# High and low parts of K and Q made in place, five steps ahead, with only the second head's rows moved

## The chip, the cores and the metric

One core of a Trainium2 chip runs the whole program. TensorE multiplies matrices, VectorE and ScalarE work on tiles in SBUF and PSUM, GpSimd works on tiles in SBUF, and SyncE (SP) issues the transfers: loads from HBM and moves from one place in SBUF to another. All of SP's transfers run on the core's 16 DMA engines. The metric is the device time in microseconds, the median of several runs.

## The reference

Attention with a forget gate over 4 batches x 8 heads, 576 positions, head size 64, and two feed-forward layers behind it over all 2304 positions:

```python
scores = scale * np.matmul(q, k.transpose(0, 1, 3, 2))
cum = np.cumsum(np.log(np.clip(f, 0.0001, 1.0)), axis=-1)
decay = cum[:, :, :, None] - cum[:, :, None, :]
scores = np.where(causal, -1e9, scores + decay)      # causal: above the diagonal
attn = softmax(scores)                               # row by row
x = attn @ v                                         # heads side by side: (2304, 512)
h = x @ w_in;  x = (h - tanh(h)) @ w_out             # w_in 512x2048, w_out 2048x512
h = x @ w2_in; out = silu(h) @ w2_out
```

All in float32. The kernel splits each factor of a product into a high part and a low part (the rest), and adds the products high x high, high x low and low x high.

## The kernel before, in words

**Pairs and steps.** The 32 heads are worked on as 16 pairs (two heads, 64 partitions each). A pair is nine tiles of scores: four row blocks of head 0, one tile that holds the last 64 rows of both heads, four row blocks of head 1. One loop takes one tile per step, and within a step each engine has work of several tiles: at step n TensorE transposes tile n-9 and computes the scores of tile n+2, ScalarE takes the exponentials of tile n-1, VectorE the row minimum of tile n and the evacuation of transposed tiles, GpSimd normalises tiles n-5 to n-3 every third step. So the normalised tiles are wanted by TensorE four steps later at the soonest, and pair p's first score is at step 9p-2. PSUM has three buffers for transposed tiles (`ps_t`): TensorE can transpose a new one only when VectorE has evacuated the third before it.

**Operands of the scores.** From pair 2 on, a score tile is two matmuls, one of `kqa` (`ta`) and one of `kqb` (`tb`), each [128, 2 heads, 1280 columns], K in columns 64 to 639, Q behind it. For head h, `ta` holds in its upper 64 partitions the high parts of K and Q, in its lower 64 the low part of K and the high part of Q; `tb` holds the high part of K and the low part of Q, and in partitions 64 to 67 four rows of decay. There are two sets (`kqt`), used by even and odd pairs. Pairs 0 and 1 use the same memory in another form (`plain`): whole high and low parts side by side, four matmuls a tile.

**How a pair is prepared.** `load_kq` loads K and Q of both heads in one transfer into `kqraw` (two buffers). `split(p, 0)` and `split(p, 1)` cast the high part into `kqhi` (K on GpSimd, Q on VectorE), `split(p, 2..5)` subtract it for the low part into `kqlo` (GpSimd, four pieces). `kqhi` and `kqlo` have one buffer each. `place` then moves the parts by DMA, six moves out of `kqhi` and four out of `kqlo`, to their places in `ta` and `tb`, and two transfers bring the decay rows from DRAM (`dec`). A table (`prep`) gives for each of these the step, relative to step 9p, at which the work for pair p+1 is issued; each engine runs its own instructions in the order of issue. A pair's operand set is free when the pair before the previous one has had its last score, at step 9p-3; head 0's half of it is free from step 9p-6 on, when the tile with the last rows is through.

**The other transfers on SP's queue.** At step 9p+1 the K/Q load of two pairs on, at step 9p+6 a V load (three buffers; it waits for the values' matmuls of an older pair), and at steps 27, 36, 45, 54, 90, 99, 135, 137 one 512 KB load of feed-forward weights each. SP issues strictly in order: an instruction that waits holds up all that stand behind it. Each transfer also uses one of eight semaphores in turn, and so waits for the eighth before it.

Of the kernel before, what the change touches and what calls it, by code (L numbers as in the profile page):

```python
# [8 lines left out]
F32R = mybir.dt.float32r  # L9
# [5 lines left out]
P = 128  # L15
# [25 lines left out]
def forgetting_attention_two_ffn(  # L41
# [286 lines left out]
    def attention():  # L328
        with ExitStack() as actx:
# [18 lines left out]
            NP = B * NPAIR  # L348
            raw, vraw, kqs, vals = {}, {}, {}, {}
            kqt = []  # L350
            for i in range(2):
                ta = kp.tile([P, 2, W], F32R, name=f"kqa{i}")
                tb = kp.tile([P, 2, W], F32R, name=f"kqb{i}")
                kqt.append((ta, tb))
# [30 lines left out]
            def split(p, j):  # L385
                if p not in kqs:
                    kqs[p] = plain[p][0:2] if p < 2 else [
                        rq.tile([P, RAW], F32R, tag=tag, name=f"{tag}{p}") for tag in ("kqhi", "kqlo")
                    ]
                hi, lo = kqs[p]  # L390
                if j == 0 and p > 1:
                    nc.gpsimd.tensor_scalar(hi[:, 0:S], raw[p][:, 0:S], 1.0, 1.0, ALU.mult, ALU.mult)
                elif j < 2:
                    c = KQ if j == 0 else slice(S, RAW)
                    (nc.vector.tensor_copy if p else nc.scalar.copy)(hi[:, c], raw[p][:, c])
                else:
                    c0, c1 = ((0, 288), (288, S), (S, S + 320), (S + 320, RAW))[j - 2]
                    sub(lo[:, c0:c1], raw[p][:, c0:c1], rd(hi[:, c0:c1]))

# [26 lines left out]
            def place(p, j):  # L426


                ta, tb = (rd(t) for t in kqt[p % 2])
                if j == 2:  # L430
                    src = dec[2 * p:2 * p + 2].rearrange("h r w -> r h w")
                    if p < 4:

                        nc.vector.memset(tb[64:68, :, Z1:Q1], 0.0)
                    nc.sync.dma_start(out=tb[64:68, :, K0:Z1], in_=src[:, :, 0:S + 512])
                    nc.sync.dma_start(out=tb[64:68, :, Q1:W], in_=src[:, :, S + 512:2 * S])
                    return
                for h in range(2):
                    a = rd(kqs[p][j][64 * h:64 * h + 64])
                    if j == 0:  # L440
                        nc.sync.dma_start(out=ta[0:64, h, K0:W], in_=a)  # L441
                        nc.sync.dma_start(out=ta[64:128, h, Q0:W], in_=a[:, S:RAW])  # L442
                        nc.sync.dma_start(out=tb[0:64, h, K0:Q0], in_=a[:, 0:S])
                    else:
                        nc.sync.dma_start(out=ta[64:128, h, K0:Q0], in_=a[:, 0:S])
                        nc.sync.dma_start(out=tb[0:64, h, Q0:W], in_=a[:, S:RAW])

# [222 lines left out]
            for a in pt4:  # L670
# [5 lines left out]
            prep = {  # L676
                -8: [(load_kq, None)], -5: [(split, 0), (split, 1)], -4: [(split, 2)], -3: [(split, 3)],
                -2: [(split, 4), (place, 2), (place, 0)], -1: [(split, 5), (place, 1)],
                10: [(prep_v, 0)], 12: [(prep_v, 1)], 15: [(load_v, None)],
# [11 lines left out]
            for p in range(NP - 1):  # L691
                for k, items in prep.items():
                    for fn, j in items:
                        if fn is prep_v:
                            later(9 * p + k, fn, p + 1, j)
                        elif j is not None:
                            if p:
                                later(9 * p + k, fn, p + 1, j)
                        elif p + 2 < NP and (p or fn is load_v):
                            later(9 * p + k, fn, p + 2)  # L700

# [131 lines left out]
```

## Time and profile before

| | us |
|---|---|
| three timed runs | 1031.77 median (1030.31 to 1033.46) |
| the profiled execution | 1022.97 |
| its span, from the first instruction to the last | 1021.2 |
| TensorE busy in the span | 991.2 (97%) |
| attention in it | about 11 to 235 |

The views answer different questions. The busy line tells which engine is full over the span; the windows tell where it is not; the wait list tells what ended an engine's idle time; the timeline shows one such wait with its neighbours; the chain follows the work that ended last from release to release. "kqhi<-kqraw" is a tile and what it is made from; buffer numbers are left out. An instruction of SP marked SPq is an issue, not a transfer: how long a transfer takes to land is seen from who waited for it.

### The profile page before, as it was taken

What the parts mean: (1) busy time and instruction counts of PE and PEld (TensorE: products, weight loads), DVE (VectorE), ACT (ScalarE), POOL (GpSimd) and SP (SyncE); (2) the same over time, 40 slices, a digit from 0 to 9 for tenths busy, and PEclk for the clock granted to TensorE, in tenths of its full rate; (3) what the DMA queues carried; (4) which work ended last, traced back from release to release, by engine and by line L of the source; (5) the groups of instructions that cost most, each with busy time, mean ns of one, the idle gap of its engine ahead of it and who ended that gap; (6) DMA issues with size and microseconds to landing.
All of it is one profiled execution on the core that took longest, in us unless ns stands there. A gap on an engine that the chain in (4) does not pass through costs nothing.

```text
span 1021.2 us, 14016 instructions
## 1 busy us (share of the span) xinstructions
PE 991.2 (97%) x4944; PEld 828.5 (81%) x4944; DVE 597.1 (58%) x1385; ACT 492.8 (48%) x1094; POOL 202.1 (20%) x288
## 2 busy tenths in 40 slices
PE   5989989999999999999999999999999999999998
PEld 4777777877898888988888888888888888888887
DVE  6677788878686544757466674443453456633323
ACT  4678788885355342434343444343344334433222
POOL 8677888975000000000000000000000000000000
PEclk9999999999999999999999999999999999999999
DMA  5899999812221101111011220110110111001111
GB/s 154 231 256 258 226 234 268 211 49 84 82 83 42 42 1 42 62 63 42 1 42 49 77 83 1 42 41 21 63 42 1 42 42 42 1 1 42 42 41 62
DMA packets 28181, 81.78 MB, mean 80 GB/s; under 512 B 4368, under 2 KB 4368, under 8 KB 28080
## 3 DMA queue, kind: packets, MB, share of 16 engines
q1 hardware_dynamic: 28104, 80.88, 27.0%
q8 instruction: 39, 0.64, 0.3%
q14 instruction: 30, 0.25, 0.1%
q10 hardware_dynamic: 8, 0.02, 0.0%
HBM read 49.39 MB, written 5.31 MB: 54 GB/s over the span
## 4 chain that ended last, share of the span: by engine, by line
PE 85%; DMA 5%; ACT 3%; SPq 2%; POOL 2%; DVE 2%; issue 1%; DVEq 0%; POOLq 0%; ACTq 0%
PE a L315 39%; PE h L256 38%; PE out_t L600 3%; DMA kqb<-kqhi 2%; PE t L555 2%; PE s L473 2%; DMA vraw<-v 1%; ACT p L527 1%; DMA kqb<-kqlo 1%; SPq L441 1%; POOL p L541 1%; PE s L477 1%; SPq L442 1%; ACT pth L573 1%; PE s L476 1%
## 5 line engine op out<-in xcount | busy, mean ns | idle before, releaser
L256 PE MATMUL h<-xh,wh 128*128 128x512 f32 (+1 forms) x640 | 237.2, 371 | 0.0
L256 PE MATMUL h<-xl,wh 128*128 128x512 f32 (+1 forms) x640 | 235.5, 368 | 0.0
L256 PE MATMUL h<-xh,wl 128*128 128x512 f32 (+1 forms) x640 | 235.5, 368 | 0.0
L278 DVE TENSOR_TENSOR gl<-g,gh 128x512 fp32r<-128x512 f32 (+1 forms) x158 | 101.6, 643 | 101.8 <-ACT gh L274 99.8
L274 ACT CAST gh<-g 128x512 fp32r<-128x512 f32 (+1 forms) x160 | 92.6, 579 | 95.9 <-DVE g L271 93.4
L256 PEld LDWEIGHTS h<-xh,wh 128*128 128x128 f32 x640 | 120.7, 189 | 21.1 <-issue 0.7
L256 PEld LDWEIGHTS h<-xl,wh 128*128 128x128 f32 x640 | 120.7, 189 | 21.0 <-issue 0.7
L256 PEld LDWEIGHTS h<-xh,wl 128*128 128x128 f32 x640 | 120.6, 188 | 20.0
L315 PE MATMUL a<-gh,wh 128*128 128x512 f32 (+1 forms) x320 | 117.9, 369 | 0.0
L315 PE MATMUL a<-gl,wh 128*128 128x512 f32 (+1 forms) x320 | 117.8, 368 | 0.0
L315 PE MATMUL a<-gh,wl 128*128 128x512 f32 (+1 forms) x320 | 117.7, 368 | 0.0
L315 PE MATMUL a<-wh,gh 128*128 128x512 f32 x288 | 112.2, 390 | 0.0
L315 PE MATMUL a<-wl,gh 128*128 128x512 f32 x288 | 112.2, 390 | 0.0
L315 PE MATMUL a<-wh,gl 128*128 128x512 f32 x288 | 112.0, 389 | 0.0
L273 ACT ACTIVATE g<-h 128x512 f32<-128x512 f32 (+1 forms) x80 | 44.4, 555 | 113.6 <-PE h L256 98.5
L244 DVE TENSOR_TENSOR xl<-y,xh 128x512 fp32r<-128x512 f32 (+1 forms) x60 | 37.4, 638 | 96.6 <-ACT xh L242 96.6
L242 ACT CAST xh<-y 128x512 fp32r<-128x512 f32 (+1 forms) x60 | 34.2, 580 | 104.8 <-PE h L256 103.1
L527 ACT ACTIVATE p<-p,mn 128x128 f32<-128x128 f32 (+3 forms) x128 | 72.3, 565 | 9.7 <-DVE mn L511 4.8
L541 POOL TENSOR_SCALAR p<-p,sm 128x128 f32<-128x128 f32 (+3 forms) x128 | 69.9, 558 | 22.9 <-DVE sm L538 10.4
L555 PE MATMUL t<-ident,p 128*128 128x128 f32 x320 | 59.6, 285 | 12.7 <-DVE sm L534 9.2
L244 DVE TENSOR_TENSOR xl<-x,xh 128x512 fp32r<-128x512 f32 (+1 forms) x56 | 34.5, 634 | 62.2 <-ACT xh L242 62.2
L315 PEld LDWEIGHTS a<-gh,wh 128*128 128x128 f32 x320 | 60.3, 189 | 10.4 <-ACT x L611 0.4
(127 smaller groups left out, 1690.8 us busy)
## 6 DMA issues: line engine op xcount, KB each, us to landing
raw<-w_in SPq DMA_DIRECT2D x32, 512.0 KB
raw<-w_out SPq DMA_DIRECT2D x32, 512.0 KB
kqraw<-kq SPq DMA_DIRECT2D x16, 608.0 KB
kqa<-kqhi SPq DMA_DIRECT2D x28, 304.0 KB
vraw<-v SPq DMA_DIRECT2D x16, 320.0 KB
out<-ob SPq DMA_DIRECT2D x18, 256.0 KB
kqa<-kqhi SPq DMA_DIRECT2D x28, 160.0 KB
kqb<-kqlo SPq DMA_DIRECT2D x28, 160.0 KB
```

What stands on the lines that cost most here:

```text
L242: nc.scalar.copy(hi[:, :n], src[:, k, t0:t0 + n])
L244: eng.tensor_tensor(lo[:, :n], src[:, k, t0:t0 + n], rd(hi[:, :n]), ALU.subtract)
L256: nc.tensor.matmul(hp[:, :n], w[:, k * P:k * P + P], m[:, :n], start=(k == 0 and r == 0), stop=(k == NKT - 1 and r == 2),)
L273: nc.scalar.activation(g[:, :n], hp[:, :n], AF.Silu)
L274: nc.scalar.copy(gh[:, :n], g[:, :n])
L278: eng.tensor_tensor(gl[:, :n], g[:, :n], rd(gh[:, :n]), ALU.subtract)
L315: nc.tensor.matmul(dst, w, m, start=(first and r == 0), stop=(last and r == 2))
L473: nc.tensor.matmul(s[:, :n], a[:, q], b[:, 0:n], start=r == 0, stop=r == 3)
L527: nc.scalar.activation(pt[:, :w], pt[:, :w], AF.Exp, bias=mn, scale=-1.0, accum_out=sums[:, n // 3 % 5, n % 3, 0:1],)
L541: nc.gpsimd.tensor_scalar(pt[:, :w], pt[:, :w], sm[:, j:j + 1], 1.0, ALU.mult, ALU.mult)
L555: nc.tensor.transpose(tp[:, c, :], pt[:, c * P:c * P + P], ident)
L600: nc.tensor.matmul(dst, w, pt[:, 448 * c + a:448 * c + q1], start=(c == 0 and r == 0), stop=(c == last and r == len(terms) - 1),)
```

## The change

High parts of pairs 2 and up are cast straight into the first head's slot of `ta`, over all 128 partitions: the upper 64 are then in place, and head 1's, in the lower 64, are moved from there. The low part of Q goes in the same way into the first head's slot of `tb`. The low part of K goes into a new tile `klo` (one buffer). `kqhi` and `kqlo` are gone. Eight moves a pair are left of ten, in three groups with the decay rows behind them: `place(p, 0)` moves 1 to 4 (head 1's high parts, and head 0's high K into `tb`), `place(p, 1)` moves 5 and 6 (low K of head 1 and of head 0), `place(p, 2)` moves 7 and 8 (head 1's low Q; head 0's high Q into the lower half), `place(p, 3)` the decay rows. Casts and subtractions keep their count and sizes; one subtraction each is issued a step earlier, the decay rows two steps later. For pairs 2 and 3, whose sets still hold plain operands, all of it is issued three steps later, and so are the K/Q loads that wait for it.

```diff
--- before.py
+++ after.py
@@ -346,8 +346,10 @@
             ps_s = pool(early, "ps_s", 3, space=PSUM)
 
             NP = B * NPAIR
-            raw, vraw, kqs, vals = {}, {}, {}, {}
+            raw, vraw, vals = {}, {}, {}
             kqt = []
+
+            klo = rq.tile([P, S], F32R, name="klo")
             for i in range(2):
                 ta = kp.tile([P, 2, W], F32R, name=f"kqa{i}")
                 tb = kp.tile([P, 2, W], F32R, name=f"kqb{i}")
@@ -383,11 +385,13 @@
                 nc.gpsimd.tensor_tensor(out, a, b, ALU.subtract)
 
             def split(p, j):
-                if p not in kqs:
-                    kqs[p] = plain[p][0:2] if p < 2 else [
-                        rq.tile([P, RAW], F32R, tag=tag, name=f"{tag}{p}") for tag in ("kqhi", "kqlo")
-                    ]
-                hi, lo = kqs[p]
+
+
+                ta, tb = kqt[p % 2]
+                if p > 1:
+                    hi, lo = ta[:, 0, K0:W], (klo, tb[:, 0, Q0:W])
+                else:
+                    hi, lo = plain[p][0], (plain[p][1][:, 0:S], plain[p][1][:, S:RAW])
                 if j == 0 and p > 1:
                     nc.gpsimd.tensor_scalar(hi[:, 0:S], raw[p][:, 0:S], 1.0, 1.0, ALU.mult, ALU.mult)
                 elif j < 2:
@@ -395,7 +399,8 @@
                     (nc.vector.tensor_copy if p else nc.scalar.copy)(hi[:, c], raw[p][:, c])
                 else:
                     c0, c1 = ((0, 288), (288, S), (S, S + 320), (S + 320, RAW))[j - 2]
-                    sub(lo[:, c0:c1], raw[p][:, c0:c1], rd(hi[:, c0:c1]))
+                    b = S * (j > 3)
+                    sub(lo[j > 3][:, c0 - b:c1 - b], raw[p][:, c0:c1], rd(hi[:, c0:c1]))
 
             def split_last(p, j):
 
@@ -426,24 +431,26 @@
             def place(p, j):
 
 
+
                 ta, tb = (rd(t) for t in kqt[p % 2])
-                if j == 2:
-                    src = dec[2 * p:2 * p + 2].rearrange("h r w -> r h w")
-                    if p < 4:
-
-                        nc.vector.memset(tb[64:68, :, Z1:Q1], 0.0)
-                    nc.sync.dma_start(out=tb[64:68, :, K0:Z1], in_=src[:, :, 0:S + 512])
-                    nc.sync.dma_start(out=tb[64:68, :, Q1:W], in_=src[:, :, S + 512:2 * S])
+                top, end = slice(0, 64), slice(64, 128)
+                kk, qs = slice(K0, Q0), slice(Q0, W)
+                moves = (
+                    ((ta[top, 1, K0:W], ta[end, 0, K0:W]), (ta[end, 1, qs], ta[end, 0, qs]),
+                     (tb[top, 1, kk], ta[end, 0, kk]), (tb[top, 0, kk], ta[top, 0, kk])),
+                    ((ta[end, 1, kk], rd(klo[end])), (ta[end, 0, kk], rd(klo[top]))),
+                    ((tb[top, 1, qs], tb[end, 0, qs]), (ta[end, 0, qs], ta[top, 0, qs])),
+                )
+                if j < 3:
+                    for a, b in moves[j]:
+                        nc.sync.dma_start(out=a, in_=b)
                     return
-                for h in range(2):
-                    a = rd(kqs[p][j][64 * h:64 * h + 64])
-                    if j == 0:
-                        nc.sync.dma_start(out=ta[0:64, h, K0:W], in_=a)
-                        nc.sync.dma_start(out=ta[64:128, h, Q0:W], in_=a[:, S:RAW])
-                        nc.sync.dma_start(out=tb[0:64, h, K0:Q0], in_=a[:, 0:S])
-                    else:
-                        nc.sync.dma_start(out=ta[64:128, h, K0:Q0], in_=a[:, 0:S])
-                        nc.sync.dma_start(out=tb[0:64, h, Q0:W], in_=a[:, S:RAW])
+                src = dec[2 * p:2 * p + 2].rearrange("h r w -> r h w")
+                if p < 4:
+
+                    nc.vector.memset(tb[64:68, 1, Z1:Q1], 0.0)
+                nc.sync.dma_start(out=tb[64:68, :, K0:Z1], in_=src[:, :, 0:S + 512])
+                nc.sync.dma_start(out=tb[64:68, :, Q1:W], in_=src[:, :, S + 512:2 * S])
 
             def prep_v(p, j):
                 r = vraw[p].rearrange("p h (c d) -> p c h d", d=D)[:, :, 0, :]
@@ -674,8 +681,9 @@
             scores(tiles[1])
 
             prep = {
-                -8: [(load_kq, None)], -5: [(split, 0), (split, 1)], -4: [(split, 2)], -3: [(split, 3)],
-                -2: [(split, 4), (place, 2), (place, 0)], -1: [(split, 5), (place, 1)],
+                -8: [(load_kq, None)], -5: [(split, 0), (split, 1)], -4: [(split, 2)],
+                -3: [(split, 3), (split, 4)], -2: [(split, 5), (place, 0)], -1: [(place, 1)],
+                0: [(place, 2), (place, 3)],
                 10: [(prep_v, 0)], 12: [(prep_v, 1)], 15: [(load_v, None)],
             }
             due = {}
@@ -694,10 +702,11 @@
                         if fn is prep_v:
                             later(9 * p + k, fn, p + 1, j)
                         elif j is not None:
+
                             if p:
-                                later(9 * p + k, fn, p + 1, j)
+                                later(9 * p + k + (3 if p < 3 else 0), fn, p + 1, j)
                         elif p + 2 < NP and (p or fn is load_v):
-                            later(9 * p + k, fn, p + 2)
+                            later(9 * p + k + (3 if fn is load_kq and p < 4 else 0), fn, p + 2)
 
             parts = (
                 ([(0, 0), (64, 0), (64, 1)], [(64, 2), (64, 3), (64, 4)]),
```

SP's queue as built before, for pair 4 (`dec` are the decay rows; "waits" names the semaphores: an engine's for its instructions, DMAHW0 to 7 for transfers):

```order
L435 DMA kqb_103<-dec 4x2x1088 [waits DMAHW6_49,PE_49]
L436 DMA kqb_103<-dec 4x2x64 [waits DMAHW7_49]
L441 DMA kqa_102<-kqhi_608 64x1216 [waits DMAHW0_49,DVE_49,Pool_49]
L442 DMA kqa_102<-kqhi_608 64x640 [waits DMAHW1_49]
L443 DMA kqb_103<-kqhi_608 64x576 [waits DMAHW2_49]
L441 DMA kqa_102<-kqhi_608 64x1216 [waits DMAHW3_49]
L442 DMA kqa_102<-kqhi_608 64x640 [waits DMAHW4_49]
L443 DMA kqb_103<-kqhi_608 64x576 [waits DMAHW5_49]
L445 DMA kqa_102<-kqlo_609 64x576 [waits DMAHW6_49,Pool_49]
L446 DMA kqb_103<-kqlo_609 64x640 [waits DMAHW7_49,Pool_49]
L445 DMA kqa_102<-kqlo_609 64x576 [waits DMAHW0_49]
L446 DMA kqb_103<-kqlo_609 64x640 [waits DMAHW1_49]
```

And with the change, the same pair's moves 1 to 8, the decay rows, a weight load and a K/Q load:

```order
L446 DMA kqa_103<-kqa_103 64x1216 [waits DMAHW2_49,PE_49,Pool_49]
L446 DMA kqa_103<-kqa_103 64x640 [waits DMAHW3_49]
L446 DMA kqb_104<-kqa_103 64x576 [waits PE_49]
L446 DMA kqb_104<-kqa_103 64x576 [waits DMAHW5_49]
L446 DMA kqa_103<-klo 64x576 [waits DMAHW6_49,Pool_49]
L446 DMA kqa_103<-klo 64x576 [waits DMAHW7_49,DMAHW4_49,DMAHW2_49]
L446 DMA kqb_104<-kqb_104 64x640 [waits DMAHW0_49,Pool_49]
L446 DMA kqa_103<-kqa_103 64x640 [waits DMAHW3_49,DMAHW1_49]
L452 DMA kqb_104<-dec 4x2x1088 [waits DMAHW0_49]
L453 DMA kqb_104<-dec 4x2x64
L141 DMA raw_0_0_713<-w_in 128x1024
L377 DMA kqraw_729<-kq 128x1216 [waits DMAHW5_49]
```

Two moves are gone, the decay rows stand last instead of first, and the sixth move and the first decay transfer wait for the semaphores of moves just issued (DMAHW4 and DMAHW2 are those of moves 3 and 1, the decay's DMAHW0 is that of move 7), not only for the one whose turn it is.

VectorE before, around its cast of pair 6's high Q (`ptl` is an evacuation of a transposed tile, `sm` the row sums, `mn` the minimum):

```order
L511 ISA pt_0_106,mn_2_4_991<-misc,mask_132,mn_2_4_991 128x288 [waits DVE_49,PE_49]
L511 ISA mn_2_4_991 128x1
L395 CAST kqhi_994<-kqraw_740 128x640 [waits DMAHW3_49,DMAHW2_49,DMAHW4_49,DMAHW1_49,DMAHW7_49,DMAHW0_49,Pool_49]
L582 TENSOR_TENSOR ptl<-t_0_3_959,pth 128x4x128 [waits Activation_49]
L534 TENSOR_REDUCE sm_1011<-sums 128x3
```

And with the change:

```order
L518 ISA pt_0_107,mn_2_4_976<-misc,mask_133,mn_2_4_976 128x288 [waits DVE_49,PE_49]
L518 ISA mn_2_4_976 128x1
L399 CAST kqa_103<-kqraw_729 128x640 [waits DMAHW5_49,DMAHW2_49,DMAHW1_49]
L589 TENSOR_TENSOR ptl<-t_0_3_944,pth 128x4x128 [waits Activation_49]
L541 TENSOR_REDUCE sm_994<-sums 128x3
```

The cast stands in the same place. Before, it waited for the six moves out of `kqhi` of the pair before; now for its own load and for two moves of the pair two before, which used the same operand set.

## Rows read from the trace of the kernel before

**Rows 1.** The page, part 1: busy us, share of the span, instructions.
```profile
PE 991.2 (97%) x4944; PEld 828.5 (81%) x4944; DVE 597.1 (58%) x1385; ACT 492.8 (48%) x1094; POOL 202.1 (20%) x288
```

**Rows 2.** Windows: stretch, us, busy us by engine, granted clock, DMA share, GB/s.
```profile
100.00:150.00 50.00, 45.84 (x284) 38.08 (x284) 40.01 (x155) 39.10 (x122) 43.89 (x64) 0.97 0.91 231
200.00:250.00 50.00, 46.73 (x246) 36.70 (x245) 39.57 (x94) 36.14 (x87) 37.34 (x38) 1.00 0.28 92
114.50:117.50 3.00, 3.00 (x12) 2.61 (x12) 2.91 (x15) 0.92 (x3) 3.00 (x5) 0.50 0.68 149
```

**Rows 3.** Waits, 11 to 240 us: who waited for whom; us, times, longest.
```profile
PE t L555 <- DVE sm L534: 9.2, 9, 1.8
...
POOL kqhi L392 <- DMA kqb<-kqhi: 7.6, 4, 3.0
...
DVE kqhi L395 <- DMA kqa<-kqhi: 2.7, 2, 1.9
```

**Rows 4.** Timeline, 111 to 113 us: start, duration, engine, line; idle before, releaser.
```profile
111.69 0.49 DVE L395 CAST kqhi<-kqraw 128x640 fp32r<-128x640 f32 x1 [1.93 <-DMA kqa<-kqhi]
...
112.10 0.68 DVE L582 TENSOR_TENSOR ptl<-t,pth 128x512 fp32r<-128x512 f32 x1
...
112.93 0.41 PE L555 MATMUL t<-ident,p 128*128 128x128 f32 x2 [1.80 <-DVE sm L534]
```

**Rows 5.** Timeline of TensorE: the first score matmul of pairs 2, 3, 14, 15.
```profile
37.26 0.31 PE L476 MATMUL s<-kqa 128*128 128x128 f32 x1
...
48.69 0.31 PE L476 MATMUL s<-kqa 128*128 128x128 f32 x1
...
189.04 0.31 PE L476 MATMUL s<-kqa 128*128 128x128 f32 x1
...
200.44 0.31 PE L476 MATMUL s<-kqa 128*128 128x128 f32 x1
```

**Rows 6.** DMA issues: out<-in, queue, count, KB of each.
```profile
raw<-w_in SPq DMA_DIRECT2D x32, 512.0 KB
...
kqraw<-kq SPq DMA_DIRECT2D x16, 608.0 KB
...
kqa<-kqhi SPq DMA_DIRECT2D x28, 304.0 KB
...
vraw<-v SPq DMA_DIRECT2D x16, 320.0 KB
...
kqb<-kqlo SPq DMA_DIRECT2D x28, 160.0 KB
...
kqb<-kqhi SPq DMA_DIRECT2D x28, 144.0 KB
```

**Rows 7.** Timeline of SP's queue: start and duration of two issues.
```profile
37.09 0.27 SPq L435 DMA_DIRECT2D kqb<-dec  x1
...
44.24 0.59 SPq L445 DMA_DIRECT2D kqa<-kqlo  x1
```

**Rows 8.** Windows of loads alone and of moves alone.
```profile
59.00:62.00 3.00, 2.85 (x20) 2.40 (x19) 3.00 (x16) 2.57 (x10) 2.48 (x6) 1.00 0.96 336
70.00:72.00 2.00, 2.00 (x16) 1.79 (x15) 1.31 (x5) 2.00 (x6) 0.00 (x0) 1.00 0.97 238
```

**Rows 9.** Timeline, first 6 us: two issues, and their first readers.
```profile
0.74 0.39 SPq L633 DMA_DIRECT2D x<-f  x1
...
1.19 0.41 SPq L375 DMA_DIRECT2D kqraw<-kq  x1
...
2.69 0.96 DVE L112 TENSOR_SCALAR x<-x 32x576 f32<-32x576 f32 x1
...
5.46 0.67 ACT L395 CAST kqa<-kqraw 128x576 fp32r<-128x576 f32 x1 [1.10 <-DMA kqraw<-kq]
```

**Rows 10.** The chain in order of time: start, us, what.
```profile
35.89 1.14 PE s L473 x4
...
161.34 3.31 DMA kqb<-kqlo
```

## The prediction, made before the changed kernel was run

> **What bounds the kernel now.** The page first: TensorE is busy 97% of the span [rows 1], so only its idle time can be won, and nearly all of that lies in attention. The windows next: from 100 to 150 us the DMA engines are busy 0.91 of the time at 231 GB/s while TensorE has 45.84 of 50 us, from 200 to 250 us the DMA share is 0.28 [rows 2]. So attention strains the DMA queue, and the two feed-forward layers do not. The wait list then names the wait: VectorE's and GpSimd's casts into `kqhi` wait for transfers that still read that one buffer, and TensorE's transposes wait nine times, 9.2 us in all, for VectorE [rows 3]. One such case in order of time: VectorE's cast idles 1.93 us for a transfer out of `kqhi`, the evacuation of the transposed tile follows behind it, and TensorE stands 1.80 us [rows 4].
>
> Measure the loss by the first score matmul of a pair. From pair 2 to pair 3 a pair takes 48.69 - 37.26 = 11.43 us, and from 14 to 15, with no K/Q load left in the queue, 200.44 - 189.04 = 11.40: TensorE's own pace. From pair 3 to pair 15 it is 200.44 - 48.69 = 151.75 us, where 12 pairs at 11.43 would be 137.2 [rows 5]. So some 14.6 us is what DMA waits cost here, and the change can win no more than that plus small change.
>
> **The change part by part.** *The removed wait.* High parts go into the first head's slot of the pair's own operands. There are two such sets, so the casts of a pair no longer follow the transfers of the pair just before; their readers are a pair older and done. The 14.6 us of lateness loses this cause entirely.
>
> *The transfers.* Before, ten moves a pair: 2 x (304 + 160 + 144 + 144 + 160) KB = 1824 KB. After, eight: 304 + 160 + 144 + 144, then 144 + 144, then 160 + 160 = 1360 KB, a quarter less [rows 6]; the moves out of the low parts have the same two small sizes. Two issues of some 0.6 us each go too [rows 7], on a queue (SP) that is not what TensorE waits for; I count them only where they stand in the loop below. Casts and subtractions keep number and size, so VectorE, ScalarE and GpSimd gain or lose no work; that the subtractions stand one step earlier is covered by GpSimd's normalisations, which have four steps of room.
>
> *What is late next.* The moves now depend on each other. Move 6 (low K of head 0) overwrites rows that moves 1 and 3 read, so SP stands until move 3 has landed. The decay rows overwrite rows that move 7 reads, so SP stands again until move 7 has landed; and the next pair's first score needs those decay rows. Queued behind each standing instruction on SP: the other moves, the weight load, the next K/Q load, the V load, and then the next pair's move 1. Those loads, issued last, are served first of the next round, ahead of move 1. Thus a loop: loads, move 1 to 3 landed, move 6 and 7, move 7 landed, decay rows, loads.
>
> Its price. Rates: two short windows, one with loads and one with moves alone, show 336 and 238 GB/s [rows 8]. The fixed part of a landing, beyond bytes by rate: the first `f` transfer is issued at 0.74 and used at 2.69, so 72 KB take at most 1.95, of which 0.2 is bytes: 1.7 us at most. The first K/Q load, issued at 1.19 and used at 5.46, takes 4.27, of which 0.62 MB by 336 is 1.85: 2.4 us. A 160 KB move late in a row of moves takes 3.31 on the chain, of which 0.69 is bytes: 2.6 us, queueing included [rows 9, 10]. For the loads I take their own 2.4; for moves, where 2.6 has queue in it and 1.7 has not, the middle, 2.1. Then, from the issue of a weight load:
> - loads and move 1 land: 2.4 + (0.524 + 0.623 + 0.328) / 0.336 + 0.311 / 0.238 = 2.4 + 4.4 + 1.3 = 8.1 us
> - moves 2 and 3: (0.164 + 0.147) / 0.238 = 1.3
> - move 6 issued: 0.6 [rows 7]; move 7 lands 2.1 + 0.7 = 2.8 after its issue
> - two decay issues before the next load: 0.6 (one is 0.27 [rows 7])
>
> 13.4 us with a weight load in the round, 11.85 without its 1.56. Both exceed 11.43. Six rounds (after the chains of pairs 4 to 7, 11 and 12, from steps 27, 36, 45, 54, 90, 99) hold a weight load; five hold only K/Q and V; the last, with no K/Q load, runs at TensorE's 11.43. Pairs 3 to 15: 6 x 13.4 + 5 x 11.85 + 11.43 = 151.1 us, against 151.75 before. The old lateness is paid back almost to the microsecond.
>
> *The three steps' delay for pairs 2 and 3.* Their set still holds plain operands. Pair 1's last plain scores end near 35.89 + 1.14 = 37.0 [rows 10]; a cast (0.7 estimated), then 3.4 + 1.3 + 0.6 + 2.8 and the decay rows' 2.6 make 48.4, against a due 48.69 [rows 5]; GpSimd's subtractions may push that back. 0 to 1.5 us late; I take 1. Pair 2 has the longer plain pair before it and costs nothing.
>
> Sum: 151.1 - 151.75 + 1 = +0.4 us (rounded). Past pair 15 nothing differs and the shift carries to the end. The profiled execution took 1022.97 us (span 1021.2), 8.8 under the median of the timed runs, 1031.77; the difference is applied to the median: 1032.
>
> *The clock.* The granted clock is 0.50, the 1.2 GHz level, in 114.5 to 117.5 us [rows 2], just after TensorE had stood 1.80 us [rows 4]. Rounds with a weight load will idle TensorE some 2 us; a fall there slows work that has those 2 us to spare. I put nothing on it.
>
> A rule that speaks against the change: by the Trainium skill, DMA: Bandwidth & Descriptors, Two DMAs through the same engine are not ordered, a transfer that depends on an earlier one has to be held at the issuing engine until the earlier one's semaphore is complete; the queue's order is no substitute. The program's order agrees: move 6 and the decay rows carry such waits. Were order enough, a round would be 5.9 us of moves and 4.4 of loads, under 11.43, and the sum 137.2: 14.6 us faster. I go by the waits.
>
> **The rivals.** *Faster: the moves land quicker than I take.* With 1.7 for every landing a round is 13.4 - 0.7 - 0.4 = 12.3 with a weight load and below TensorE's pace without: 6 x 12.3 + 6 x 11.43 = 142.4, 9.4 us less: 1022. For it: a quarter fewer bytes, and the queue is empty when moves 6 and 7 start. Against it: the load row's 2.4. Chance 0.23.
>
> *Faster still: moves also run at the loads' rate.* With 1.7 per landing and 336 GB/s for every byte a round with a weight load is 1.7 + 4.4 + 0.93 + 0.93 + 0.6 + 1.7 + 0.49 + 0.6 = 11.35 us, under TensorE's pace: all 14.6 us won, 1018 with 1 us lost at pair 3. For it: a move alone in the queue was not seen. Against it: the 238 GB/s of the window with moves alone [rows 8]. Chance 0.03. Beside it stands the Trainium skill, DMA: Bandwidth & Descriptors, Anatomy of one DMA, whose fit (made on another issue path) is 2.0 us plus bytes at 436 GB/s; by it, as an estimate, a round is 10.4 us.
>
> *Slower: the chain of landings outweighs the removed wait.* Place: TensorE's first score of each pair, standing for the decay rows. With 2.6 for every landing a round is 13.4 + 0.2 + 0.5 = 14.1, and 12.55 without a weight load; the sum is 6 x 14.1 + 5 x 12.55 + 11.43 = 158.8, 7 us more, and with 1.5 at pair 3 8.5 us: 1040. For it: 3.31 for a small move [rows 10]; every hiccup of the queue now lies on the chain. It decides from 0.14 us more per landing (two landings in each of 11 rounds: 3.1 us). Chance 0.31.
>
> *The wait moves instead of going:* VectorE's cast still waits for its pair's K/Q load, now issued behind the decay rows. That load is issued some 2 us before a pair's first score and lands in some 4.3 [rows 9], 6 behind a weight load; the cast needs it six steps of 11.43 / 9 us, 7.6 us, after that score. Some 3.5 us to spare; it would cost about 1.5 us in each of ten rounds, 1047, if not. Chance 0.03.
>
> **How the numbers follow.** No change to be told (within 0.3%, 3.1 us, about what this kernel's measurement can tell from none): 0.40, itself 1029 to 1035. Faster 0.23 + 0.03 = 0.26, slower 0.31 + 0.03 = 0.34. The range takes in both ends of the landing time: 1023 to 1041.
>
> **What would show it.** Right: no wait of VectorE's or GpSimd's casts for a move; TensorE's waits at the first score of a pair, ended by the decay transfer; SP standing on its own transfers twice a pair; pair periods near 13.4 and 11.9; DMA share down to some 0.8. Wrong for the size: periods of 11.4 throughout (landings quicker), or over 12.5 without a weight load (slower). Wrong altogether: casts that still wait for transfers, or stalls at pairs 2 and 3 alone.

## The result, and the profile after

| | us |
|---|---|
| before, 4 timed runs | 1031.04 median (1025.1 to 1033.46) |
| changed, 4 timed runs | 1043.06 median (1041.33 to 1046.1) |
| ratio | 1.015, 95% interval 1.011 to 1.019 |
| predicted | 1032, range 1023 to 1041 |
| profiled execution of the changed kernel | 1041.33, span 1039.5 |

Slower by 1.5%, and outside the range. In a later comparison it was 1038.01 against 1028.05: 1.0098 (1.0072 to 1.0125).

The page's first line answers to [rows 1]: TensorE has 10 us more busy time (much of it at half speed, below) and 8 us more idle time.

```profile
PE 1001.2 (96%) x4944; PEld 834.4 (80%) x4944; DVE 597.0 (57%) x1385; ACT 491.0 (47%) x1094; POOL 199.5 (19%) x288
```

The first window of [rows 2] after the change (stretch, us, busy us of TensorE, its weight loads, VectorE, ScalarE, GpSimd, granted clock, DMA share, GB/s):

```profile
100.00:150.00 50.00, 42.95 (x266) 34.74 (x266) 37.72 (x149) 38.01 (x120) 39.19 (x57) 1.00 0.74 182
```

From 100 to 150 us the DMA engines are less busy than before, 0.74 against 0.91, and TensorE has less to do as well, 42.95 against 45.84 us. A quarter fewer moved bytes, and more waiting: something stands still between the transfers. The waits from 11 to 240 us (three of TensorE's, then SP's two longest; us, times, longest) say what:

```profile
PE s L484 <- DMA kqb<-dec: 14.3, 11, 1.9
PE s L480 <- POOL kqa L385: 3.1, 1, 3.1
...
PE t L562 <- DVE sm L541: 1.5, 5, 0.5
...
SPq L446 <- DMA kqb<-kqa: 33.3, 14, 5.0
SPq L452 <- DMA kqb<-kqb: 19.9, 14, 1.6
```

The 9.2 us behind VectorE of [rows 3] are down to 1.5, and no cast waits for a move. In their place TensorE stands eleven times, 14.3 us, at a pair's first score for the decay rows; SP stands once a pair for move 3 (in front of move 6) and once for move 7 (in front of the decay rows). The chain in order of time, the two links of it in one round:

```profile
75.36 2.54 DMA kqb<-kqb
77.90 0.02 issue
77.92 2.68 DMA kqb<-dec
...
80.73 0.30 PE s L484
...
90.04 2.97 DMA kqb<-kqb
93.01 0.02 issue
93.02 2.70 DMA kqb<-dec
```

Move 7 lands, the decay rows are issued 0.02 us later and land, the score starts 0.14 us after that, and 15 us on the same follows again.

The first scores answer to [rows 5]; here pairs 3 and 15:

```profile
53.88 0.30 PE L483 MATMUL s<-kqa 128*128 128x128 f32 x1
...
218.72 0.31 PE L483 MATMUL s<-kqa 128*128 128x128 f32 x1
```

The twelve pairs from 3 to 15 take 218.72 - 53.88 = 164.84 us, where they took 151.75 before and where 151.1 was predicted. The six rounds with a weight load average 14.75 us, five without one 12.98, and one runs at TensorE's pace: not the last, as predicted, which took 12.77, but the first, from pair 3 to 4, 11.40. In addition pair 3 starts 5.2 us later than in [rows 5]. The two together, 13.1 + 5.2, are the 18.3 us between the spans of the two profiles.

### The profile page after: what moved, and what is told of

Read it like the earlier page. It is cut to its first block, busy times and chain, and to the rows that moved or that the text cites. A ratio compares the mean times of both kernels' runs of the same rounds, so it can differ in the third digit from the quotient of the medians.

```text
span 1039.5 us, 13899 instructions
## 1 busy us (share of the span) xinstructions
PE 1001.2 (96%) x4944; PEld 834.4 (80%) x4944; DVE 597.0 (57%) x1385; ACT 491.0 (47%) x1094; POOL 199.5 (19%) x288
## 3 DMA queue, kind: packets, MB, share of 16 engines
HBM read 49.39 MB, written 5.31 MB: 53 GB/s over the span
## 4 chain that ended last, share of the span: by engine, by line
PE 83%; DMA 9%; POOL 3%; ACT 2%; issue 1%; DVE 1%; SPq 0%; POOLq 0%; ACTq 0%
PE a L315 38%; PE h L256 37%; PE out_t L607 2%; DMA kqb<-kqb 2%; DMA kqb<-dec 2%; DMA kqb<-kqa 2%; PE s L480 2%; PE t L562 1%; POOL p L548 1%; DMA vraw<-v 1%; DMA kqa<-klo 1%; ACT p L534 1%; PE s L484 1%; DMA raw<-w_out 0%; SPq L446 0%
## 5 line engine op out<-in xcount | busy, mean ns | idle before, releaser
L315 PEld LDWEIGHTS a<-gh,wh 128*128 128x128 f32 x320 | 60.3, 189 | 10.3 <-ACT x L618 0.4
L315 PEld LDWEIGHTS a<-gh,wl 128*128 128x128 f32 x320 | 60.3, 189 | 10.1
```

The costliest lines, as they stand in the source:

```text
L315: nc.tensor.matmul(dst, w, m, start=(first and r == 0), stop=(last and r == 2))
```

## The experiments

All numbers on one measure: the start of the first score of pair 3, and the twelve pairs from there to pair 15, read as above in each trace. TensorE's own pace would be 137.2. "Full" is when TensorE's weight loads fall from 0.33 to 0.19 us. The unchanged kernel was timed anew beside each group of kernels, with medians of 1031.04, 1029.73, 1026.23 and 1028.05, and the ratios are to the one beside; compare ratios rather than medians. The last three columns are from one execution each. Two executions of one kernel differ by 3.1 us (before) and 1.3 us (changed) in the twelve pairs, so a smaller difference there tells nothing by itself.

| kernel | median us | ratio to before, 95% | full at us | pair 3 at | twelve pairs |
|---|---|---|---|---|---|
| before | 1031.04 | | 32 | 48.69 | 151.75 |
| before, second profile | 1032.32 (one run) | | 47 | 54.90 | 154.87 |
| changed | 1043.06 | 1.011 to 1.019 | 44 | 53.88 | 164.84 |
| changed, again | 1038.01 | 1.0072 to 1.0125 | 46 | 54.76 | 163.54 |
| low Q aside, decay rows free | 1028.87 | 0.9952 to 1.0015 | 46 | 54.68 | 151.60 |
| loads on ScalarE's queue | 1038.21 | 1.0053 to 1.0125 | 44 | 53.76 | 165.33 |
| before, two `kqhi` | 1040.57 | 1.0073 to 1.0161 | 31 | 48.91 | 167.27 |
| changed, other order | 1024.08 | 0.9943 to 1.0007 | 32 | 49.39 | 150.76 |
| low Q aside, other order | 1017.12 | 0.9849 to 0.9933 | 32 | 48.23 | 147.52 |
| changed, no V loads | 1027.79 | 0.9977 to 1.0046 | 32 | 48.57 | 154.70 |
| K and low parts aside | 1022.14 | 0.9928 to 0.9992 | 32 | 48.45 | 147.55 |
| weight loads spread | 1015.67 | 0.9863 to 0.9918 | 31 | 48.21 | 144.67 |
| and high Q on ScalarE | 1011.16 | 0.9814 to 0.9873 | 47 | 54.87 | 140.14 |

**Low Q aside.** Is the wait of the decay rows the price? Low K and Q into one tile, one move more, decay rows first (left out here: the slices of `klo` in moves 5 and 6, and the zeros now set for both heads):

```diff
-            klo = rq.tile([P, S], F32R, name="klo")
+            klo = rq.tile([P, RAW], F32R, name="klo")
-                    hi, lo = ta[:, 0, K0:W], (klo, tb[:, 0, Q0:W])
+                    hi, lo = ta[:, 0, K0:W], (klo[:, 0:S], klo[:, S:RAW])
-                    ((tb[top, 1, qs], tb[end, 0, qs]), (ta[end, 0, qs], ta[top, 0, qs])),
+                    ((tb[top, 1, qs], rd(klo[end, S:RAW])), (tb[top, 0, qs], rd(klo[top, S:RAW])), (ta[end, 0, qs], ta[top, 0, qs])),
-                -3: [(split, 3), (split, 4)], -2: [(split, 5), (place, 0)], -1: [(place, 1)],
-                0: [(place, 2), (place, 3)],
+                -3: [(split, 3), (split, 4)], -2: [(split, 5), (place, 3), (place, 0)], -1: [(place, 1)],
+                0: [(place, 2)],
```

> The changed kernel with the low parts of K and Q in one tile aside (nine moves a pair, 1520 KB), so that the decay rows wait for no move and are issued first of a pair's transfers; the sixth move still waits for moves 1 and 3. Measure: the time from the first score of pair 3 to that of pair 15, 164.84 us in the changed kernel, 151.75 in the kernel before, 137.2 at TensorE's own pace. Theory 1, the loop of landings bounds: a round loses one landing with its issues, some 2.6 us, so rounds fall from 14.75 to about 12.1 with a weight load and from 12.98 to TensorE's 11.43 without; twelve pairs take 140 to 145 us, no first score waits for the decay rows, and the time falls by 20 to 25 us to about 1020. Rival 2, the DMA engines' bytes bound: 160 KB more a pair can only cost, 165 us or more, 1043 or more. Rival 3, TensorE's late rise to its full clock and the two falls are the loss: 12 pairs stay near 160.

13.2 us of the twelve pairs went, with 160 KB more per pair, and no first score waits for decay rows any more. So the wait has a price, and more bytes did not undo the gain. But 151.60 is above the expected 140 to 145, and the time fell by 12 to 17 us by the ratios, not 20 to 25: SP still stands for move 3, as its queue shows in a round without a weight load (start, duration of the issue, what):

```profile
118.18 0.59 SPq L377 DMA_DIRECT2D kqraw<-kq  x1
...
124.36 2.98 SPq L446 DMA_DIRECT2D kqa<-klo  x2
127.43 1.20 SPq L446 DMA_DIRECT2D kqb<-klo  x2
128.68 0.59 SPq L446 DMA_DIRECT2D kqa<-kqa  x1
129.32 0.59 SPq L377 DMA_DIRECT2D kqraw<-kq  x1
```

From load to load 11.1 us; in weight rounds of the same kernel 13.1 to 14.8.

**Loads on another queue.**

```diff
-                nc.sync.dma_start(out=raw[p], in_=kq[b, hp])
+                (nc.sync if p < 4 else nc.scalar).dma_start(out=raw[p], in_=kq[b, hp])
```

(and so for V and for the weights of attention.)

> The changed kernel with the K/Q and V loads of pairs 4 and up and the weight loads of attention issued on ScalarE's queue; moves and decay rows stay alone on SyncE's. Theory 1: the loads leave the loop; the chain from a pair's first move to its decay rows took 10.9 us where nothing stood ahead of it (40.94 to 51.84 us in the changed kernel), under 11.43, so if the two queues do not slow each other the twelve pairs take 137 to 140 us and the time is near 1017; if they share the engines byte by byte a round is still 10.9 plus part of the 4 to 6 us of loads and the twelve pairs take 150 to 165. Rival 2, bytes bound whatever the queue: 165, 1043. ScalarE pays some 0.4 us an issue, 26 issues, beside its own idle time.

No gain: 165.33. A load issued by ScalarE still delays moves issued by SP. SP's queue in one round, with ScalarE's two issues set behind it:

```profile
88.69 0.59 SPq L446 DMA_DIRECT2D kqb<-kqb  x1
89.37 0.55 SPq L446 DMA_DIRECT2D kqa<-kqa  x1
95.98 0.25 SPq L452 DMA_DIRECT2D kqb<-dec  x1
```
```profile
85.84 0.35 ACTq L141 DMA_DIRECT2D raw<-w_in  x1
87.66 0.33 ACTq L377 DMA_DIRECT2D kqraw<-kq  x1
```

Move 7, issued at 88.69, lets the decay rows go at 95.98: 7.3 us instead of some 2.6, and the K/Q load issued one microsecond before it, on the other queue, landed in that time, at 95.32 by its semaphore. So a dependent move that finds a load ahead of it is late here, whichever queue the load came from.

**The cast's wait alone.** Two buffers of `kqhi`, the ten moves as before; for room the low parts are written over the loaded K and Q:

```diff
-                        rq.tile([P, RAW], F32R, tag=tag, name=f"{tag}{p}") for tag in ("kqhi", "kqlo")
-                    ]
+                        rq.tile([P, RAW], F32R, tag="kqhi", name=f"kqhi{p}", bufs=2), raw[p].bitcast(F32R)]
```

> The kernel before with two buffers of the tile that holds the high parts (the low parts written over the loaded K and Q to make room); the ten moves and their order stay. Only the casts' wait for the previous pair's transfers is gone. If that wait was what made 151.75 us of the twelve pairs (what the prediction took): 137.2, some 14 us faster than before, 1017. If the bytes of ten moves and the loads fill the queue, and the wait only showed it: 2752 KB a round at 238 GB/s for the moves and 215 to 336 for the loads are 10.7 to 12.3 us, 1.6 more with a weight load, so 150 or more, no change from before.

It tells less than it should. It was 11 us slower than before, but the edit made a wait of its own: SP's K/Q load now stands for the moves out of the buffer that it fills, issued just before.

```profile
SPq L375 <- DMA kqb<-kqraw: 27.0, 13, 3.8
```

That left the question open; "K and low parts aside" asks it again.

**Before, a second profile.**

> The kernel before, unchanged, for a second profile of it. In its first profile TensorE's matmuls and weight loads run at half speed up to 32.21 us, in the changed kernel's up to 44.06 us, and the first score of pair 3 stands at 48.69 and 53.88 us. If the late rise belongs to the change (its stalls or its order), this profile rises near 32 again; if it is chance from run to run, it may rise anywhere up to 44 us and its first score of pair 3 moves with it by up to 5 us.

The 5 us at pair 3 are not the change's. The unchanged kernel starts pair 3 at 54.90 here, later than the changed one at 53.88. What differs from its first profile is TensorE's speed at the start. A weight load of 128 x 128 in the second profile, just before and just after:

```profile
45.91 0.33 PEld L600 LDWEIGHTS out_t<-ptl,vhl 128*128 128x128 f32 x1
...
47.02 0.19 PEld L476 LDWEIGHTS s<-kqa 128*128 128x128 f32 x1
```

**The changed kernel in another order.** Its eight moves, same operands and bytes, in the order 3, 1, 2, 4, 7, 5, 6, then the decay rows, then move 8:

```diff
-                    ((ta[top, 1, K0:W], ta[end, 0, K0:W]), (ta[end, 1, qs], ta[end, 0, qs]),
-                     (tb[top, 1, kk], ta[end, 0, kk]), (tb[top, 0, kk], ta[top, 0, kk])),
-                    ((ta[end, 1, kk], rd(klo[end])), (ta[end, 0, kk], rd(klo[top]))),
-                    ((tb[top, 1, qs], tb[end, 0, qs]), (ta[end, 0, qs], ta[top, 0, qs])),
+                    ((tb[top, 1, kk], ta[end, 0, kk]), (ta[top, 1, K0:W], ta[end, 0, K0:W]),
+                     (ta[end, 1, qs], ta[end, 0, qs])),
+                    ((tb[top, 0, kk], ta[top, 0, kk]), (tb[top, 1, qs], tb[end, 0, qs]), (ta[end, 1, kk], rd(klo[end]))),
+                    ((ta[end, 0, kk], rd(klo[top])),),
+                    ((ta[end, 0, qs], ta[top, 0, qs]),),
-                if j < 3:
+                if j < 4:
-                0: [(place, 2), (place, 3)],
+                0: [(place, 2), (place, 4), (place, 3)],
```

> The changed kernel with its eight moves in another order on SyncE's queue and nothing else: moves 3, 1, 2, then 4, 7, 5, then 6, the decay rows, 8. Same operands, same bytes. Move 7 now lands beside moves 1 to 5, so the decay rows find it landed, and only move 6 stands. Theory 1, the loop of landings bounds: a round is loads to landing of moves 3 and 1 (9.6 + about 0.3 us with a weight load, 8.2 + 0.3 without, measured in the changed kernel) plus some 1.9 of issues, 11.8 and 10.4, so only weight rounds stay above TensorE's 11.43: the twelve pairs take 138 to 142 us against 164.85, and the time falls by 22 to 26 us to about 1018, below the kernel before. Rival, the engines' bytes or the clock bound: within 5 us of the changed kernel's 1043.

This is the run that settles the cause: the order of SP's issues alone is worth 14 us of the twelve pairs, and the time is 0.9975 of the kernel before, where it was 1.0098 and 1.015. The first scores of pairs 3 and 15:

```profile
49.39 0.30 PE L484 MATMUL s<-kqa 128*128 128x128 f32 x1 [0.45 <-DVE ptf L593]
...
200.15 0.30 PE L484 MATMUL s<-kqa 128*128 128x128 f32 x1
```

It missed the expected 138 to 142: the decay rows still find move 7 in flight, 13.2 us in all where it was 19.9 (one move 7, issued at 90.71 behind loads and five moves, lands at 97.44, 6.7 us later, where the one of the chain above took 2.5).

```profile
SPq L447 <- DMA kqa<-kqa: 22.9, 10, 4.8
SPq L453 <- DMA kqb<-kqb: 13.2, 14, 1.6
```

**The low Q aside, in another order.** The kernel of the first experiment, with moves 3 and 1 first and move 6 last but one.

> The kernel of the first experiment (low Q aside, nine moves, decay rows first) with the sixth move put behind all others but the eighth, and the third first. SyncE still stands for move 3 and 1, but the other moves fill the DMA engines meanwhile. Theory 1: the loop is loads to landing of moves 3 and 1, then two issues, 10.9 us with a weight load and 9.5 without, all under 11.43: twelve pairs 137 to 140 us, time near 1015. Its 160 KB more a pair would show against the other order of the changed kernel only if the engines were full: then 142 to 146.

It beats both kernels: 1.1% faster than before. The decay rows free and move 6 late: 147.52, still above the expected 137 to 140 and above the 142 to 146 for full engines. What is left above 137.2: 6.2 us from pair 5 to pair 8, behind four weight loads in a row, 2.4 between pairs 8 and 9 (below), and 1.6 in the rounds of pairs 10 and 12.

**Without V loads.**

```diff
-                vraw[p] = vp.tile([P, 2, 5 * D], F32, tag="vraw", name=f"vraw{p}", bufs=3)
-                nc.sync.dma_start(out=vraw[p], in_=v[b, hp])
+                vraw[p] = vp.tile([P, 2, 5 * D], F32, tag="vraw", name=f"vraw{p}", bufs=3) if p < 4 else vraw[3]
+                if p < 4:
+                    nc.sync.dma_start(out=vraw[p], in_=v[b, hp])
```

> The changed kernel without the V loads of pairs 4 and up (they use pair 3's V). A V load took 1.7 to 2.1 us between the landing of the K/Q load and its own in the changed kernel, where the prediction's 336 GB/s gives it 0.98. If its time in the loop is what the trace shows, each of eleven rounds shortens by about 2.0 us: weight rounds from 14.75 to 12.75, the others from 12.98 to 11.43 (TensorE's pace, 1.5 less): twelve pairs 164.85 - 12 - 7.8 = 145. If 0.98 is right: 164.85 - 11 = 154. If the loads are beside the loop: no change.

154.70, 10 us less than the changed kernel: the 154 that followed from 0.98 us a load, not the 145 from 2.0. From decay issue to decay issue the weight rounds went from 14.71 to 13.67 on average, the others from 13.32 to 11.84: 1.0 and 1.5 us. Yet V's landing did come 1.7 to 2.1 us behind that of K/Q. The times between two landings do not add up: without V, the K/Q load behind a weight load lands 2.4 to 3.5 us after it, with V 2.0 to 3.2, where 0.623 / 0.336 = 1.85 was counted. In both kernels the load that stands right before the moves is the slow one, be it V or K/Q.

**K and low parts aside.** High K in a tile of two buffers, low K and Q in one, only high Q in place: ten moves, none that waits for one just issued but the last.

> High K aside in two buffers and low parts aside; only the high Q in place: ten moves, 1664 KB, no move waits for the landing of one just issued except the last, which has six in between. The casts wait for no transfer of the pair just before. It asks again what the earlier experiment with two buffers left open, since there the K/Q load had to wait for moves out of its own buffer. If landings alone bound the loop: twelve pairs 137 to 141 us, time near 1016. If the engines' bytes bound: 1664 KB at 230 GB/s are 7.4 us, K/Q and V 4.4, a weight load 1.5, so 11.8 and 13.3 a round: twelve pairs 150 us, near the kernel before, and 1360 KB win by bytes.

147.55, with 1664 KB. Neither the casts' wait nor the loop is left, and the twelve pairs are 4 us shorter than before (0.996 in time), not 14. That speaks for most of what [rows 5] lose not being that wait, but does not show it: this kernel has losses of its own, such as one stand of 3.1 us of a first score for a move. The kernel with low Q aside in its other order, with 1520 KB, took the same 147.52: between these two, bytes do not tell.

**The last two** spread the weight loads over every second round, and then move the cast of high Q from VectorE to ScalarE:

```diff
-            for n, k, m in ((27, 0, 0), (36, 0, 1), (45, 1, 0), (54, 1, 1), (90, 2, 0), (99, 2, 1),
+            for n, k, m in ((18, 0, 0), (36, 0, 1), (54, 1, 0), (72, 1, 1), (90, 2, 0), (108, 2, 1),
```
```diff
-                    (nc.vector.tensor_copy if p else nc.scalar.copy)(hi[:, c], raw[p][:, c])
+                    (nc.vector.tensor_copy if p == 1 else nc.scalar.copy)(hi[:, c], raw[p][:, c])
```

> The nine-move kernel in its second order, with the six weight loads of attention in every second round (steps 18, 36, 54, 72, 90, 108) instead of four in a row and two. In the second-order kernel the rounds with a weight load took 12.0, 12.8 and 14.5 us from load to load, those without 10.3; four in a row let the transfers fall behind by some 6 us, one at a time lets them catch up. If so the twelve pairs take 140 to 143 us instead of 147.5 and the time falls by 5 us to about 1012. If the loss there is VectorE's cast (3.29 us at 120.45, where it is 0.49 elsewhere) or the clock: no change from 1017.

> The same with the cast of the high part of Q on ScalarE for pairs 2 and up, not on VectorE. In the second-order kernel VectorE's cast lasts 3.29 us while GpSimd works without a break from 117.71 to 123.38, and TensorE then stands 2.23 us. If the cast waits for GpSimd, ScalarE's does not: that stall goes, 2 us less than the kernel with spread weight loads. If ScalarE's work (0.7 us a pair more) delays its exponentials instead: the same or 2 to 5 us more.

144.67 and 140.14: the best kernel of the study is 1.6% faster than before (0.9844, 0.9814 to 0.9873). The spread alone does not show in the time: its ratio is 0.9891, as without it. The rounds from pair 5 to 8 are 5.4 us shorter, as expected, but the one from 9 to 10 took 13.04 us instead of 11.39, behind TensorE's stand for VectorE's cast and with the granted clock at 0.50, the 1.2 GHz level, from 120.23 us for 3.4. With the cast on ScalarE both losses are gone, 4.5 us in all where 2 were expected. Its window from 100 to 150 us:

```profile
100.00:150.00 50.00, 49.27 (x316) 40.45 (x315) 41.27 (x169) 46.81 (x143) 48.06 (x70) 1.00 0.90 248
```

TensorE has 49.27 of 50 us, and the DMA engines are as busy as before the change: a full queue as in [rows 2] costs little when TensorE waits for nothing in it.

**The changed kernel again.**

> The changed kernel again, on the same chip as the two above. Theory 1: its first score of pair 3 comes near 48.7 or near 54 us, as TensorE's full clock comes near 32 or 45 us, by chance as in the kernel before; the twelve pairs take 160 to 168 us either way. Rival (the three steps' delay costs 5 us at pair 3): 53 to 54 us with an early full clock too.

Twelve pairs 163.54, pair 3 at 54.76 with the full clock at 46: the loop repeats, and this run alone does not refute the rival. The other runs do: five kernels with the same three steps' delay start pair 3 at 48.2 to 49.4 where the clock came at 31 to 32.

## Why the prediction was wrong

The loop that the prediction described is there, link for link; the likeliest case took it too short, and so did the rival that had the right sign (1040, chance 0.31).

*The step that failed* is "loads and move 1 land: 2.4 + (0.524 + 0.623 + 0.328) / 0.336 + ...": one rate for all loads. Here is a weight round of the changed kernel on SP's queue:

```profile
77.92 0.27 SPq L452 DMA_DIRECT2D kqb<-dec  x1
...
78.57 0.36 SPq L141 DMA_DIRECT2D raw<-w_out  x1
78.97 0.43 SPq L377 DMA_DIRECT2D kqraw<-kq  x1
79.51 0.36 SPq L382 DMA_DIRECT2D vraw<-v  x1
79.98 1.12 SPq L446 DMA_DIRECT2D kqa<-kqa  x2
81.19 2.58 SPq L446 DMA_DIRECT2D kqb<-kqa  x2
83.86 6.08 SPq L446 DMA_DIRECT2D kqa<-klo  x2
90.04 0.82 SPq L446 DMA_DIRECT2D kqb<-kqb  x1
...
93.02 0.28 SPq L452 DMA_DIRECT2D kqb<-dec  x1
```

| link, weight rounds | predicted | measured, mean of 6 | this round |
|---|---|---|---|
| first load issued, to move 6 issued | 9.4 | 10.8 | 10.9 |
| to decay rows issued | 3.4 | 3.2 | 3.5 |
| to the next load | 0.6 | 0.7 | 0.7 |
| round | 13.4 | 14.7 | 15.1 |

(The pair of issues at 83.86 ends at 89.94, and an issue behind a wait takes some 0.46, so move 6 starts at 89.48.) The second and third link came out within 0.2 us. The four rounds with a K/Q load and no weight load repeat it: 9.4 measured for the first link, 7.84 counted. All of the error of these ten rounds, 1.3 to 1.5 us each, is in the first link, where loads and moves share the engines. By the landings it sits at V: in the round shown, K/Q has landed 6.1 us after the first issue (5.8 counted), V after 8.2 (6.8), move 1 after 9.5 (8.1). Behind the K/Q load issued at 33.30 us, with no moves behind it, V had landed 0.8 us after K/Q; here it takes 2.1.

Two of the six rounds, those with first loads at 107.61 and 177.33, have more in them, which the mean hides. SP stood there for the values of an older pair before it could issue the V load and move 1:

```profile
SPq L382 <- ACT tmp L622: 3.8, 2, 1.9
```

And of the sixteen updates of K/Q's semaphore that tell of its landing, the last came 2.0 and 3.0 us after the fifteenth. The two longest loads of instructions in attention (16 KB, 1.8 and 1.7 us) stand in the trace beside these two; that they are the reason is not shown. The other four rounds have 10.5 us for the first link.

The windows of one such burst, at 66 to 74 us, and of a K/Q and a V load that had nothing behind them, at 35 to 37:

```profile
66.00:68.00 2.00, 2.00 (x14) 1.84 (x15) 2.00 (x10) 1.05 (x5) 2.00 (x3) 1.00 1.04 373
68.00:70.00 2.00, 1.88 (x14) 1.43 (x13) 0.94 (x5) 1.26 (x3) 2.00 (x4) 1.00 0.91 228
70.00:72.00 2.00, 1.99 (x12) 1.52 (x13) 1.27 (x8) 1.17 (x5) 1.03 (x3) 1.00 1.03 265
72.00:74.00 2.00, 1.93 (x12) 1.21 (x10) 1.03 (x3) 1.83 (x7) 2.00 (x4) 1.00 0.94 211
...
35.00:37.00 2.00, 2.00 (x8) 1.45 (x8) 1.48 (x8) 1.65 (x8) 1.39 (x3) 1.00 1.00 393
```

The weight load and the first half of K/Q run at 373 GB/s, the rest of K/Q, V and the first of move 1 at 228 to 265, and K/Q and V with nothing behind them at 393. By 246, the mean of the two, instead of 336, K/Q and V cost 0.951 / 0.246 = 3.9 us instead of 2.8, and move 1 by 211 instead of 238 1.5 instead of 1.3: 1.2 us of the 1.3 to 1.5. The trace of before had it: the window that gave 336 [rows 8] held the weight load and most of K/Q, and the same burst went on like this:

```profile
62.00:64.00 2.00, 2.00 (x19) 1.97 (x17) 1.11 (x8) 0.64 (x3) 2.00 (x3) 1.00 0.97 288
64.00:66.00 2.00, 1.87 (x11) 1.11 (x9) 1.55 (x6) 1.84 (x6) 2.00 (x4) 1.00 1.03 176
66.00:68.00 2.00, 2.00 (x13) 1.39 (x11) 0.40 (x3) 0.15 (x1) 1.48 (x4) 1.00 1.00 210
```

A rate was read from the best three microseconds of ten. What slows the loads, the moves' own packets or something else, no run here settles.

*The other points.*
- The removed wait: right that the casts stop waiting. That all 14.6 us were its was never shown, and the runs speak against it: [rows 3] has six waits of casts for moves, 10.3 us, and ten moves without that wait and without the loop won 4 us.
- The three steps' delay, +1 us: 48.2 to 49.4 where before had 48.69, so nothing to be told from none.
- The clock, put at nothing: the two stalls of 1.72 us at 80.73 and 179.44 were each followed by 3.4 us at the granted clock 0.50, the 1.2 GHz level. Stalls of 1.92 and 1.61 us at 165.09 and 109.67 were not. The rounds that hold the two falls, 15.3 and 16.2 us, are the longest together with another of 15.3 that has none. An estimate of what a fall costs is 1.7 us, from the 13.04 and 11.39 of the round from pair 9 to 10 above; two are 3.4 at most, of 13.7 missed. It can add, and is not the cause.
- Going by the waits was right: SP stood 33.3 and 19.9 us for moves 3 and 7. The Trainium skill, DMA: Bandwidth & Descriptors, Two DMAs through the same engine are not ordered, asks for this wait on the earlier transfer's semaphore at the issuing engine. No run here leaves a wait out, so none shows what the queue's order alone would do.
- "The wait moves to the K/Q load", chance 0.03: no cast waited for its load.
- The bound of the range, 1041, came from landings of 2.6 us with loads at 336; with 228, 1.34 us more in each of eleven rounds, it would have stood 14.7 us higher and held the result.

## What to carry to other kernels

Making operands in place saves a tile and a move, but turns independent transfers into a chain of landings; count the landings between the first and the last transfer of a round and compare them with the round before counting bytes. Where a queue issues in order, put the transfers that others wait for first and those that must wait last: here that alone was worth 14 us of 165. And read a transfer's rate from the whole burst in which it will stand, not from its best window.

## What the runs showed of the hardware

**The start of TensorE's full speed varies from run to run.** One kernel reached it at 32 us in one execution and at 47 in the next; pair 3 then starts 6 us later. The durations of weight loads, 0.33 and 0.19 us, show it, and the record of the granted clock begins there, at 32.21 and 46.65 us, with 1.00, the 2.4 GHz level. Before that the trace has no record, and the column reads 1.00 for want of one. In the second execution TensorE was busy for all of 35 to 45 us, and still slow. The late start is probably in many of the spreads above: the best kernel has 1011.0 to 1017.5, and its one profile, of the 1017.5, reached full speed at 47.

**VectorE's cast waits inside its own duration.** In the kernel with low Q aside in its second order, one cast of 128 x 640, 0.49 us in [rows 4], lasts 3.29, and TensorE then stands 2.23 us:

```profile
120.45 3.29 DVE L399 CAST kqa<-kqraw 128x640 fp32r<-128x640 f32 x1
...
124.48 0.41 PE L562 MATMUL t<-ident,p 128*128 128x128 f32 x2 [2.23 <-DVE sm L541]
```

GpSimd worked over that time without a break:

```profile
120.64 0.87 POOL L385 TENSOR_TENSOR vhl<-vraw,vhl 128x320 fp32r<-128x320 f32 x1
121.48 0.68 POOL L396 TENSOR_SCALAR kqa<-kqraw 128x576 fp32r<-128x576 f32 x1
122.12 1.26 POOL L177 TENSOR_TENSOR wl<-wa,wh 128x512 fp32r<-128x512 f32 x1
```

The cast ends 0.36 us after GpSimd's last. With the cast on ScalarE the stall was gone (round of pairs 8 to 9, weight loads spread: 11.42 us instead of 14.18). The kernel before has it too: its cast at 136.39 us lasts 2.25. The Trainium skill, SBUF — State Buffer, SBUF: two separate sides, describes a port pair that either VectorE, in some modes, or GpSimd holds for a whole instruction while the other is blocked. The trace is in keeping with it, though here the cast waits over several of GpSimd's instructions in a row. The profile counts such a wait as busy time, with no releaser.
